# Where the weight sums of a later expert pair stand among the evictions of a batch's first second-layer product

## Chip, cores and metric

The kernel runs on one core of a Trainium2 chip. The metric is the device time of one execution in microseconds, given as the median of several runs. Five engines work on their own instruction queues and meet at semaphores: TensorE (PE, matmuls, and PEld, its weight loads), VectorE (DVE), ScalarE (ACT), GpSimd (POOL) and SyncE (SP, which issues the transfers here).

## What is computed

Three stages follow one another: clustered attention, a gated layer, and a mixture of four experts. The change lies in the last one, so only that is shown:

```python
def _moe2_ref(x, domain_probs, w1, w2):          # x: 1536 x 512, w1: 4 x 512 x 1024, w2: 4 x 1024 x 512
    p = domain_probs / (domain_probs.sum(-1, keepdims=True) + 1e-09)
    out = np.zeros((N, D), dtype=np.float32)
    for e in range(E):
        h = np.maximum(x @ w1[e], 0.0)
        out += p[:, e:e + 1] * (h @ w2[e])
    return out
```

## The kernel before

The stage (`moe2`) walks over 32 pairs: 2 batches of 768 tokens, 4 experts, 4 groups of 256 hidden units. A pair has a first layer, `hidden(i)`, and a second layer, `outp(i)`. The order of the instructions on each engine is the order in which the Python code issues them, since the stage stands under a manual schedule.

`hidden(i)` computes 256 hidden units for 768 tokens by a scheme with seven products of blocks instead of eight. Each product is six matmuls (two halves of the depth, and three terms, because every number is split into a high and a low part). The products go into four PSUM banks, `ph0` to `ph3`, one buffer each. The first product (line 886) is copied out by ScalarE as `m1` (line 887); the sums `u2` and `u3` are formed by VectorE (lines 890 and 893). The fifth product issued (line 899) adds into the bank of the first, so it comes behind the copy `m1`; the sixth (line 903) writes the bank that `u2` read. ReLU and the split into high and low parts are ScalarE's and VectorE's (lines 877 and 878).

`outp(i)` multiplies the hidden units with the second layer's weights in six tiles of 128 tokens. A tile is six matmuls of 512 columns (lines 931 to 933) into one of four `po` buffers in PSUM; VectorE evicts it, scaled by the token's share of the expert. The first pair of a batch writes the accumulator (line 936), the others add to it (line 938). So tile 4 needs the buffer of tile 0, and tile 5 that of tile 1.

Two lists of side work are woven in. `conv_in2(i)` prepares the first layer's weights of pair i: an entry with four sums on VectorE into the tile `sf` (line 828), and four entries, each a ScalarE copy that makes the high part (line 835) and a GpSimd subtraction that makes the low part (line 836), of which two read `sf`. `sf` has one buffer, so the sums of one pair come behind the subtractions of the pair before. `conv_out2` does the same for the second layer's weights (lines 614 and 615). `outp` takes one entry of its list behind each eviction (lines 942 and 943), and issues what is left behind its loop (lines 944 and 945).

The loop over i (lines 950 to 965) issues the load of pair i+2, `hidden(i)`, and then `outp(i-1)` with the list of pair i+2. At i = 0 and i = 16 there is no `outp`; the list of pair i+2 is kept as `late`, and goes into `hidden(1)` or `hidden(17)` behind its own work, whose last entries are issued at its end (lines 910 and 911). So in `hidden(1)` pair 2's weights are prepared, and in `outp(0)`, which follows, pair 3's. In the second batch it is `hidden(17)` with pair 18 and `outp(16)` with pair 19.

Of the kernel before, what the change touches and what calls it, by code (L numbers as in the profile page):

```python
# [69 lines left out]
class Net:  # L70
# [781 lines left out]
    def moe2(self):  # L852
        nc = self.nc
        pairs, hs, acc = self.pairs2, {}, {}
        LAST, PER = len(pairs), len(pairs) // B
# [57 lines left out]
        def outp(i, work=()):  # L913
            work = list(work)
            b, e, g = pairs[i]
            first, last = i % PER == 0, i % PER == PER - 1
            if first:
                acc[b] = self.a2p.tile([128, NT, DM], F32, name="acc2", tag="acc2") if b == 0 else \
                    self.accp.tile([128, NT, DM], F32, name="acc3", tag="acc")
            Hh, Hl = hs.pop(i)  # L920
            wo = self.wout2.pop(i)
            for t in range(NT):

                parts = (slice(0, 256), slice(256, 512)) if i == LAST - 1 and t == NT - 1 else (slice(0, 512),)
                c = slice(t * 128, t * 128 + 128)
                pe = self.pn[:, b, t, e:e + 1]
                for dc in parts:
                    ps = self.ps3.tile([128, 512], F32, name="po2", tag="po")[:, 0:dc.stop - dc.start]
                    for f in range(2):
                        wh, wl = wo[f]  # L930
                        nc.tensor.matmul(ps, Hh[:, f, c], wh[:, dc], start=f == 0, stop=False)  # L931
                        nc.tensor.matmul(ps, Hh[:, f, c], wl[:, dc], start=False, stop=False)  # L932
                        nc.tensor.matmul(ps, Hl[:, f, c], wh[:, dc], start=False, stop=f == 1)  # L933
                    a = acc[b][:, t, dc]
                    if first:
                        nc.vector.tensor_scalar(a, ps, pe, None, op0=ALU.mult)  # L936
                    else:
                        nc.vector.scalar_tensor_tensor(a, ps, pe, a, op0=ALU.mult, op1=ALU.add)  # L938
                    if last:
                        o = self.out[b * S:(b + 1) * S].rearrange("(p t) d -> p t d", t=NT)[:, t, dc]  # L940
                        nc.sync.dma_start(out=o, in_=a)
                if work:
                    work.pop(0)()
            for go in work:
                go()


        sums, split = self.operands(1, [self.block(0, k, n) for k in range(2) for n in range(2)])
        late = []
        for i in range(LAST):  # L950
            if i + 2 < LAST:
                self.load_in2(i + 2)
            hidden(i, (self.conv_out2(i + 1) if i + 1 < LAST else []) + late)
            late = []
            cin = self.conv_in2(i + 2) if i + 2 < LAST else []
            if i + 2 < LAST:
                self.load_out2(i + 2)
            if i == PER - 1:

                outp(i - 1, [lambda o=o: split(o, nc.gpsimd if o in (1, 3) else nc.vector) for o in (0, 4, 1, 5)] + cin[:1])  # L960
                outp(i, [lambda: split(3, nc.gpsimd), lambda: split(6), lambda: split(2)] + cin[1:])
            elif i == 0 or i == PER:
                late = cin
            else:
                outp(i - 1, cin + (sums[i - 2:i - 1] if 2 <= i < 6 else []))
        outp(LAST - 1)

    def run(self):
# [85 lines left out]
```

## Time and profile before

| | us |
|---|---|
| median of 3 runs | 1085.11 (1084.38 to 1086.39) |
| the profiled execution | 1084.51 |
| its span on the core | 1082.6 |
| TensorE busy in the span | 1051.1 (97%) |
| VectorE busy in the span | 773.5 (71%) |
| mean granted TensorE clock, as a share of full speed | 0.991 |

The span is what the trace covers; 1.9 us of the execution lie around it. Times in the rows count from the span's start. A timeline row gives start, length, engine, line, operation, what is written from what, how many instructions were merged into the row, and in brackets the idle time before it with what ended it. Matmuls overlap, so a matmul's length is more than the distance to the next start.

### The profile page before, as it was taken

To read this page: it belongs to the slowest core of one execution; us is meant where nothing else is said; L and a number is where in the kernel's file an instruction comes from. 1 tells how busy PE (TensorE), PEld (TensorE's weight loads), DVE (VectorE), ACT (ScalarE), POOL (GpSimd) and SP (SyncE) were. 2 spreads that over 40 slices of the span, in tenths; PEclk is the share of its full clock that TensorE was granted. 3 is DMA by queue.
4 is the path that set the end of the run, shared out by engine and by line. 5 is a ranking of instruction groups with operands and counts; after the bars stand their busy time and mean duration, and the time that the engine had idled before them with its cause. 6 is when DMAs were issued, how large, how long until landed. Compare 5 with 4: busy or idle time off the path is not lost.

```text
span 1082.6 us, 15421 instructions
## 1 busy us (share of the span) xinstructions
PE 1051.1 (97%) x5621; PEld 947.8 (88%) x5621; DVE 773.5 (71%) x1315; ACT 512.0 (47%) x1060; POOL 465.2 (43%) x398
## 2 busy tenths in 40 slices
PE   6999999999999999999999999999999899999998
PEld 5898999998888888888898888998899798899887
DVE  6998989998877526644357777667768767776765
ACT  4888888888665315503224333333343333333320
POOL 7577787763333103100025444444435544444430
PEclk8999999999999999999999999999999899999999
DMA  8678667655433202102012122212213212221201
GB/s 176 136 160 174 143 150 169 149 131 162 147 117 98 78 1 95 61 1 68 11 40 66 52 78 78 67 50 78 79 59 117 76 42 78 78 72 46 78 20 59
DMA packets 92619, 95.80 MB, mean 88 GB/s; under 512 B 42720, under 2 KB 71744, under 8 KB 92544
## 3 DMA queue, kind: packets, MB, share of 16 engines
q1 hardware_dynamic: 92112, 94.77, 32.2%
q8 instruction: 44, 0.72, 0.3%
q14 instruction: 31, 0.25, 0.1%
q10 hardware_dynamic: 432, 0.06, 0.0%
HBM read 65.07 MB, written 3.19 MB: 63 GB/s over the span
## 4 chain that ended last, share of the span: by engine, by line
PE 83%; DVE 7%; DMA 4%; ACT 3%; POOL 2%; issue 1%; SPq 1%; ACTq 0%; POOLq 0%
PE ph L869 20%; PE po L931 8%; PE po L932 8%; PE po L933 8%; PE S L421 4%; PE T L441 4%; PE pg L621 3%; PE pg L623 3%; PE pv L623 3%; PE pv L621 3%; PE pv L622 3%; PE pg L622 3%; PE po L621 3%; PE po L623 3%; PE po L622 3%; DMA R<-hik 2%
## 5 line engine op out<-in xcount | busy, mean ns | idle before, releaser
L869 PE MATMUL ph<-X,w1h 128*128 128x384 f32 x896 | 229.2, 337 | 0.1
L869 PEld LDWEIGHTS ph<-X,w1h 128*128 128x128 f32 x896 | 163.5, 189 | 3.3 <-DVE h2l L878 0.8
L931 PE MATMUL po<-woh,h2h 128*128 128x512 f32 (+1 forms) x386 | 151.2, 392 | 7.3 <-DVE acc L936 7.3
L938 DVE SCALAR_TENSOR_TENSOR acc<-po,pn,acc 128x512 f32<-128x512 f32 (+1 forms) x181 | 129.8, 742 | 36.3 <-PE po L933 36.3
L615 POOL TENSOR_TENSOR wol<-r,woh 128x512 fp32r<-128x512 f32 x64 | 83.3, 1303 | 168.5 <-ACT woh L614 168.5
L933 PE MATMUL po<-woh,h2l 128*128 128x512 f32 (+1 forms) x386 | 151.5, 392 | 0.0
L932 PE MATMUL po<-wol,h2h 128*128 128x512 f32 (+1 forms) x386 | 151.4, 392 | 0.0
L869 PE MATMUL ph<-X,w1l 128*128 128x384 f32 x448 | 150.6, 336 | 0.0
L596 POOL TENSOR_TENSOR cvc<-cvc,cvs 128x512 int32<-128x512 int32 x36 | 49.5, 1380 | 197.2 <-DVE cvc L593 192.5
L877 ACT ACTIVATE h2h<-ph 128x384 fp32r<-128x384 f32 x128 | 62.6, 490 | 117.5 <-PE ph L869 91.7
L445 DVE TENSOR_TENSOR pl<-T,ph 128x384 fp32r<-128x384 f32 x192 | 97.0, 547 | 13.8 <-ACT ph L444 12.0
L836 POOL TENSOR_TENSOR w1l<-sf,w1h 128x512 fp32r<-128x512 f32 x64 | 81.5, 1296 | 48.1 <-ACT w1h L835 48.1
L836 POOL TENSOR_TENSOR w1l<-r,w1h 128x512 fp32r<-128x512 f32 x64 | 66.9, 1047 | 80.3 <-ACT w1h L835 80.3
L878 DVE SCALAR_TENSOR_TENSOR h2l<-ph,h2h 128x384 fp32r<-128x384 f32 x128 | 71.0, 554 | 34.5 <-ACT h2h L877 31.4
L931 PEld LDWEIGHTS po<-woh,h2h 128*128 128x128 f32 x386 | 73.1, 189 | 22.5 <-DVE acc L936 8.2
L424 DVE TENSOR_REDUCE nm<-S 128x1 f32<-128x768 f32 x96 | 91.1, 949 | 2.0 <-PE S L421 1.1
L421 PE MATMUL S<-R,L 80*128 80x384 f32 (+1 forms) x384 | 92.0, 362 | 0.0
L444 ACT ACTIVATE ph<-T 128x384 fp32r<-128x384 f32 x192 | 84.2, 493 | 16.1 <-PE T L441 15.4
L432 ACT ACTIVATE P<-S,nm 128x768 f32<-128x768 f32 x96 | 87.5, 911 | 3.8 <-DVE nm L424 3.8
L933 PEld LDWEIGHTS po<-woh,h2l 128*128 128x128 f32 x386 | 73.1, 189 | 15.2
L932 PEld LDWEIGHTS po<-wol,h2h 128*128 128x128 f32 x386 | 73.1, 189 | 14.3
L441 PE MATMUL T<-ident,P 128*128 128x128 f32 x576 | 82.4, 277 | 2.8 <-DVE pl L445 2.5
(183 smaller groups left out, 2281.1 us busy)
## 6 DMA issues: line engine op xcount, KB each, us to landing
r<-in_moe_w_dram SPq DMA_DIRECT2D x64, 512.0 KB, 3.8
L<-hiq SPq DMA_DIRECT2D x32, 192.0 KB, 4.7
R<-hik SPq DMA_DIRECT2D x32, 192.0 KB, 4.7
wo<-in_moe_w_out_dram SPq DMA_DIRECT2D x12, 512.0 KB, 3.4
wv<-in_moe_w_val_dram SPq DMA_DIRECT2D x12, 512.0 KB, 4.0
wg<-in_moe_w_gate_dram SPq DMA_DIRECT2D x12, 512.0 KB, 4.6
nq<-in_q_dram SPq DMA_DIRECT2D x16, 192.0 KB, 4.0
nk<-in_k_dram SPq DMA_DIRECT2D x16, 192.0 KB, 4.1
```

The lines of the kernel that those rows point to most:

```text
L421: nc.tensor.matmul(ps[:, a, 0:384], l[0:k, c], r[0:k, a * 384:a * 384 + 384], start=l is L1, stop=l is L2)
L441: nc.tensor.transpose(ps[:, j, :], pt[:, c:c + 128], self.ident)
L445: nc.vector.tensor_tensor(lo, ps, hi.bitcast(F32), op=ALU.subtract)
L621: nc.tensor.matmul(ps, wh, xh, start=first, stop=False)
L622: nc.tensor.matmul(ps, wh, xl, start=False, stop=False)
L623: nc.tensor.matmul(ps, wl, xh, start=False, stop=last)
L836: nc.gpsimd.tensor_tensor(lo[:, sl], x, hi[:, sl].bitcast(F32), op=ALU.subtract)
L869: nc.tensor.matmul(ps, w[:, a, j], y[:, o, j], start=first and j == 0 and k == 0, stop=j == 1 and k == 2, skip_group_check=not first)
L931: nc.tensor.matmul(ps, Hh[:, f, c], wh[:, dc], start=f == 0, stop=False)
L932: nc.tensor.matmul(ps, Hh[:, f, c], wl[:, dc], start=False, stop=False)
L933: nc.tensor.matmul(ps, Hl[:, f, c], wh[:, dc], start=False, stop=f == 1)
L938: nc.vector.scalar_tensor_tensor(a, ps, pe, a, op0=ALU.mult, op1=ALU.add)
```

## The change

In the two calls `outp(0)` (i = 1) and `outp(16)` (i = 17) three empty entries are put ahead of the list. `outp` takes one entry behind each eviction, so the four sums are issued behind the fourth eviction instead of the first, the first weight split behind the fifth and the second behind the sixth, and the last two splits behind the loop. All other calls of `outp` keep their lists.

```diff
@@ -962,7 +962,9 @@
             elif i == 0 or i == PER:
                 late = cin
             else:
-                outp(i - 1, cin + (sums[i - 2:i - 1] if 2 <= i < 6 else []))
+
+                gap = [lambda: None] * (3 if i in (1, PER + 1) else 0)
+                outp(i - 1, gap + cin + (sums[i - 2:i - 1] if 2 <= i < 6 else []))
         outp(LAST - 1)
```

## Rows read from the trace of the kernel before

**Rows 1.** The page's first part: busy us, share of the span, instructions of each engine.

```profile
PE 1051.1 (97%) x5621; PEld 947.8 (88%) x5621; DVE 773.5 (71%) x1315; ACT 512.0 (47%) x1060; POOL 465.2 (43%) x398
```

**Rows 2.** TensorE's waits, whole run: line, releaser, us in total, times, longest.

```profile
PE po L931 <- DVE acc L936: 7.3, 2, 3.7
...
```

**Rows 3.** Busy time and granted clock (PEclk) from one `outp` start to the next.

```profile
core 0: us, PE busy (x) PEld busy (x) DVE busy (x) ACT busy (x) POOL busy (x), PEclk, DMA share, GB/s
585.83:606.60 20.77, 17.09 (x80) 14.97 (x80) 14.20 (x24) 7.57 (x16) 12.17 (x11) 0.92 0.16 51
606.60:622.11 15.51, 15.51 (x80) 14.07 (x80) 11.82 (x21) 5.49 (x12) 7.13 (x7) 1.00 0.23 69
839.53:861.36 21.83, 18.16 (x79) 16.03 (x79) 14.20 (x24) 7.56 (x16) 11.87 (x11) 0.84 0.14 49
861.36:876.87 15.51, 15.51 (x80) 14.07 (x79) 10.95 (x20) 5.49 (x12) 7.13 (x7) 1.00 0.22 68
...
```

**Rows 4.** TensorE's timeline at `outp(0)`: end of tile 4, tile 5, `hidden(2)`.

```profile
592.44 0.39 PE L933 MATMUL po<-woh,h2l 128*128 128x512 f32 x1
596.51 0.79 PE L931 MATMUL po<-woh,h2h 128*128 128x512 f32 x1 [3.67 <-DVE acc L936]
...
599.23 0.59 PE L869 MATMUL ph<-X,w1h 128*128 128x384 f32 x2
...
```

**Rows 5.** TensorE's timeline, an undisturbed pair: first matmuls of `hidden(3)` and of `outp(2)`.

```profile
614.80 0.51 PE L869 MATMUL ph<-X,w1h 128*128 128x384 f32 x2
...
622.10 0.39 PE L931 MATMUL po<-woh,h2h 128*128 128x512 f32 x1
...
```

**Rows 6.** TensorE's timeline at `outp(16)`: end of tile 4, tile 5, `hidden(18)`.

```profile
846.14 0.39 PE L933 MATMUL po<-woh,h2l 128*128 128x512 f32 x1
850.21 0.79 PE L931 MATMUL po<-woh,h2h 128*128 128x512 f32 x1 [3.67 <-DVE acc L936]
...
852.93 0.84 PE L869 MATMUL ph<-X,w1h 128*128 128x384 f32 x2
...
```

**Rows 7.** VectorE's timeline from the end of `hidden(1)` to the sums of pair 4.

```profile
588.07 1.39 DVE L828 TENSOR_TENSOR sf<-sf,r 128x256 f32<-128x256 f32 x1
...
590.05 0.74 DVE L936 TENSOR_SCALAR acc<-po,pn 128x512 f32<-128x512 f32 x1
592.79 0.93 DVE L828 TENSOR_TENSOR sf<-r 128x256 f32<-128x256 f32 x1 [2.00 <-POOL w1l L836]
593.75 1.37 DVE L828 TENSOR_TENSOR sf<-sf,r 128x256 f32<-128x256 f32 x1
...
595.72 2.71 DVE L936 TENSOR_SCALAR acc<-po,pn 128x512 f32<-128x512 f32 x4
...
609.05 1.01 DVE L828 TENSOR_TENSOR sf<-r 128x256 f32<-128x256 f32 x1
...
```

**Rows 8.** GpSimd's timeline at `outp(0)`.

```profile
590.20 2.56 POOL L836 TENSOR_TENSOR w1l<-sf,w1h 128x512 fp32r<-128x512 f32 x2 [1.03 <-ACT w1h L835]
...
595.86 2.51 POOL L836 TENSOR_TENSOR w1l<-sf,w1h 128x512 fp32r<-128x512 f32 x2 [1.02 <-ACT w1h L835]
598.33 0.72 POOL L836 TENSOR_TENSOR w1l<-r,w1h 128x256 fp32r<-128x256 f32 x1
...
```

**Rows 9.** The sums' line 828, whole run: ns min/median/max, and VectorE's idle before it.

```profile
L828 DVE TENSOR_TENSOR sf<-sf,r x32: 424/426/1391, 541.0 to 1035.4; 128x256 f32<-128x256 f32 x32
...
  POOL w1l L836: 4.0, 2
...
```

**Rows 10.** ScalarE's timeline at `outp(0)` and the start of `hidden(2)`.

```profile
595.15 1.30 ACT L835 ACTIVATE w1h<-sf 128x512 fp32r<-128x512 f32 x2 [3.53 <-DVE sf L828]
596.36 0.40 ACT L835 ACTIVATE w1h<-r 128x256 fp32r<-128x256 f32 x1
600.55 0.49 ACT L887 ACTIVATE m<-ph 128x384 f32<-128x384 f32 x1 [3.79 <-PE ph L869]
...
```

**Rows 11.** SyncE's queue: the load of pair 4's first-layer weights.

```profile
593.47 0.37 SPq L808 DMA_DIRECT2D r<-in_moe_w_dram  x1
...
```

**Rows 12.** The page's transfers, whole run: count, KB each, median us to landing.

```profile
r<-in_moe_w_dram SPq DMA_DIRECT2D x64, 512.0 KB, 3.8
...
```

## What the change should do to the time

> **What bounds the kernel now.** I read the page's table of busy shares first [rows 1]: TensorE is busy in 97% of the span and no other engine above 71%, so time can come back only where TensorE stands still or runs at its lower clock. Next the list of waits of TensorE, longest first [rows 2]: its head is a matmul of the second layer that waits for an eviction of line 936, 7.3 us in 2 times. Line 936 evicts only the first pair of a batch, so the two times should be the first second-layer product of each batch, `outp(0)` and `outp(16)`. To size the whole loss I then cut the span from the start of one `outp` to the start of the next [rows 3]. An undisturbed cut is 15.51 us, in both batches, at a granted clock of 1.00; the two cuts that begin at `outp(0)` and `outp(16)` are 20.77 and 21.83 us at 0.92 and 0.84. The excess is 5.26 and 6.32 us, 11.58 us in all. That is more than the wait, so I split it by the timelines of TensorE.
>
> First place [rows 4]: the last matmul of tile 4 starts at 592.44. An undisturbed tile of `outp` takes (614.80 - 606.60)/6 = 1.367 us [rows 3, 5], a matmul of it 0.228, so tile 5 was due at 592.67; it starts at 596.51, 3.84 late. Tile 5 itself takes 596.51 to 599.23 = 2.72 us, twice 1.367: the lower of the clock's two levels, 1.2 instead of 2.4 GHz, right behind an idle of 3.67 us. The following `hidden(2)` lasts to 606.60, 7.37 against 622.10 - 614.80 = 7.30 [rows 3 to 5]. Sum 3.84 + 1.35 + 0.07 = 5.26. Second place [rows 6]: tile 5 was due at 846.37, starts at 850.21 (3.84), takes 2.72 (1.35 too much), and `hidden(18)` 852.93 to 861.36 = 8.43 (1.13 too much): 6.32. Of the 11.58 us, 7.68 are idle and 3.90 the clock behind it.
>
> Why tile 5 waits: `po` has four buffers, so tile 5 needs the eviction of tile 1. VectorE's timeline [rows 7] shows eviction 0 at 590.05, then nothing until 592.79, then the four weight sums of pair 3, and only at 595.72 the evictions 1 to 4. The sums waited for GpSimd, whose two splits of pair 2 that read the one `sf` buffer run 590.20 to 592.76 [rows 8]; over the run this wait counts 4.0 us in 2 times [rows 9]. Eviction 1 ends at about 595.72 + 0.74 = 596.46, and TensorE goes on at 596.51.
>
> **The change, part by part.** Nothing is added: the three empty entries issue no instruction. In `outp(0)` and `outp(16)` the sums go behind eviction 3, the first split behind eviction 4, the second behind eviction 5, the last two behind the loop. The splits are ScalarE copies and GpSimd subtractions; neither engine has anything else in `outp`, so the order inside both queues is what it was. SyncE's queue is untouched too. What changes is VectorE's order alone: four sums trade places with evictions 1 to 3.
>
> Evictions 1 to 3 no longer stand behind the sums. The block of four takes 2.71 us [rows 7]; as one of them is 0.74 long, each starts (2.71 - 0.74)/3 = 0.66 behind the other. So 590.05, 590.71, 591.37, 592.03, and the last ends at 592.77. Their tiles are there: tile 3 begins 3 x 1.367 behind the cut at 585.83 [rows 3], and its last matmul ends near 591.5. Tile 5 is due at 592.67 and needs eviction 1, done at 591.45: 1.2 us of slack. The wait goes in full. With the idle gone the clock has no reason to fall: from `outp(1)` on, without an idle, it is 1.00 [rows 3]. Gain 5.26 and 6.32 us. As the second place has 1.06 us of clock cost more at the same idle, another execution may have it the other way: 2 x 5.26 = 10.5 to 2 x 6.32 = 12.6 are the ends for this term; I take the measured sum, 11.58.
>
> What the sums pay: nothing. They could not start before GpSimd's end at 592.76, whoever stands ahead of them, and eviction 3 ends at 592.77. So they run 592.79 to 595.72 as before, cover and price unchanged, and eviction 4 begins at 595.72, eviction 5 at 596.38 (end 597.12).
>
> What is late next is `hidden(2)`, which TensorE now starts at 592.67 + 1.37 = 594.04 instead of 599.23, while ScalarE and VectorE are still at the sums' consequences. Each product of six matmuls takes 7.30/7 = 1.043 us. On ScalarE, pair 3's splits keep their times, 595.15 to 596.76 [rows 10]; the copy `m` of the first product stands behind them in the queue and runs 596.77 to 597.26 (0.49 [rows 10]). TensorE needs it for the fifth product, which adds into the same bank, at 594.04 + 4 x 1.043 = 598.21: 0.95 us of slack. VectorE does `u2` behind both `m` and eviction 5, 597.3 to 597.9; the sixth product, into the bank `u2` reads, is due at 599.25: 1.4 us of slack. So the covers hold, but the smallest is under 1 us. If evictions and splits slow each other, it is this slack that is eaten first.
>
> That can be bounded by rows. A VectorE sum with two inputs in SBUF does collide with GpSimd: 1.39 us at 588.07 where others take 0.42 [rows 7, 9]. Evictions read PSUM, and do not: the block of four runs at 595.72 to 598.43 beside two GpSimd splits that take 2.51 us, where two splits with only one eviction beside them took 2.56 [rows 7, 8]. I take zero, the row of exactly this pair of operations. The upper end is that GpSimd is locked out for three evictions, 3 x 0.66 = 2.0 us: the sums begin 2.0 later, `m` too, and TensorE loses 2.0 - 0.95 = 1.05 us per place. The lower end (a gain) is excluded, since GpSimd's times set the sums either way.
>
> The Trainium skill, page "SBUF — State Buffer" (section on the two separate sides), says that VectorE and GpSimd share a port pair as an exclusive lock, held by whichever begins first, for two-input SBUF operations and the two-port modes. Read for the sums it agrees with the 1.39 us row; read for every VectorE operation it would be the upper end above, but the same page exempts an operation with at most one SBUF input outside those modes, and the 2.51 us row agrees with the exemption. By the lock the sum would be 9.5 us of gain, by the exemption 11.6.
>
> Transfers: pair 4's weights are issued at 593.47, when GpSimd has freed the buffer, and land in about 3.8 us [rows 11, 12], near 597.3; their sums move from 609.05 [rows 7] to 603.8. Hidden by 6 us. GpSimd, which ends pair 3's splits at 599.05 as before [rows 8], falls behind `hidden(2)` by at most 2 to 3 us; in an undisturbed cut it is busy 7.13 of 15.51 us [rows 3], so it catches up in the same pair.
>
> Sum: 1084.51 (the profiled execution, span 1082.6 and 1.9 around it) - 11.58 = 1072.93. The median of the three runs is 1085.11, 0.60 above this execution: 1073.5 from there. I say 1073.2.
>
> **The rivals.** (a) GpSimd is held up by the evictions and `hidden` gives 1.05 us back at each place: 11.58 - 2.1 = 9.5, time 1075.0 to 1075.6. For it: the two do collide in sums. Against: the 2.51 us row. (b) Only the idle goes and the clock falls anyway, since something else lowers it: gain 7.7, time 1076.8 to 1077.4. Against: 1.00 in the undisturbed cuts. (c) No change: tile 5 does not wait for eviction 1 but for something that also waits for GpSimd; then the idle stays and the time is 1085. Against: 596.46 and 596.51 agree within 0.05 us, and the sums had ended 0.7 us before. (d) Slower: the wait moves from tile 5 into `hidden`. `m` stands behind the splits that stand behind the sums; if the sums end late, TensorE idles at the fifth product, and the clock falls in front of 18 matmuls of `hidden` and 36 of `outp`. At an idle of 5 us and 1.35 to 2.48 us for the clock as now, each place would cost 6.4 to 7.5 where it costs 5.26 and 6.32 today: 1 to 3.4 us slower in all, 1086 to 1088.5. It decides from the point where `m` ends 0.95 + 5 = 6 us later than 597.26. For it: `hidden` now overlaps the sums, which it did not before. Against: nothing in GpSimd's or ScalarE's queue moves.
>
> **How the numbers follow.** Forecast (whole gain) 0.84, (a) 0.08, (b) 0.04, (c) 0.02, (d) 0.02. A measurement of this kernel tells about 0.2%, 2.2 us, from no change; forecast, (a) and (b) are all faster than that: 0.96; (c) within 0.2% with the mild part of (d): 0.03; slower 0.01. Low end: the lowest run, 1084.38, less 12.6 = 1071.8. High end: the highest run, 1086.39, less 9.4 = 1077.0, which takes in (a) and most of (b).
>
> **What would show it.** Right: no wait of TensorE for line 936; four evictions in a row ahead of the sums, the sums still at GpSimd's end; both cuts near 15.5 us at a clock of 1.00. Wrong in (a): splits longer than 1.3 us each beside evictions and an idle ahead of the fifth product of `hidden(2)`. Wrong in (b): matmuls of 0.63 us in `outp(0)` without an idle ahead. Wrong in (d): a wait of TensorE for ScalarE's `m` or VectorE's `u`, with half-clock matmuls behind it.

## The result, and the profile after

| | before | after |
|---|---|---|
| median, us | 1085.75 (1084.38 to 1087.13, 4 runs) | 1073.18 (1071.80 to 1075.07, 4 runs) |
| ratio | | 0.9887, 95% interval 0.9859 to 0.9915 |
| the profiled execution and its span, us | 1084.51, 1082.6 | 1073.04, 1071.1 |
| mean granted TensorE clock | 0.991 | 0.996 |

The change takes 1.1% off. By the medians that is 12.57 us, by the two profiled executions 11.47; the runs of either kernel spread over some 3 us. TensorE's waits over the whole run (line, releaser, us in total, times, longest) now begin with entries of the attention stage; the wait for line 936 that headed [rows 2] is in the list no more:

```profile
PE oT L364 <- DVE oh L358: 5.0, 1, 5.0
PE PV L454 <- ACT U L461: 5.0, 7, 1.2
...
```

The same cuts as in [rows 3], from one `outp` start to the next, of the changed kernel (length, busy time and count of PE, PEld, DVE, ACT, POOL, then the clock):

```profile
585.85:601.35 15.50, 15.50 (x79) 14.05 (x79) 14.14 (x24) 7.45 (x16) 12.29 (x11) 1.00 0.20 69
601.35:616.86 15.51, 15.51 (x79) 14.06 (x79) 11.81 (x21) 5.48 (x12) 7.12 (x7) 1.00 0.23 69
834.31:849.82 15.51, 15.51 (x79) 14.06 (x79) 14.15 (x24) 7.46 (x16) 11.93 (x11) 1.00 0.21 69
849.82:865.33 15.51, 15.51 (x80) 14.07 (x80) 10.94 (x20) 5.48 (x12) 7.11 (x7) 1.00 0.22 68
...
```

The cuts of `outp(0)` and `outp(16)` are as long as the undisturbed ones, with TensorE busy all through and the clock at 1.00. They lost 20.77 - 15.50 = 5.27 and 21.83 - 15.51 = 6.32 us, together 11.59, where the span lost 11.5. Nothing of it came back later: VectorE is busy 14.14 us of the first cut, as much as before, but no longer in TensorE's way.

TensorE's timeline at `outp(0)` (answers to [rows 4]): end of tile 4, tile 5, first and fifth product of `hidden(2)`, and the start of `outp(1)`:

```profile
592.46 0.39 PE L933 MATMUL po<-woh,h2l 128*128 128x512 f32 x1
592.69 0.39 PE L931 MATMUL po<-woh,h2h 128*128 128x512 f32 x1
...
594.05 0.51 PE L869 MATMUL ph<-X,w1h 128*128 128x384 f32 x2
...
598.23 0.51 PE L869 MATMUL ph<-X,w1h 128*128 128x384 f32 x2
...
601.35 0.39 PE L931 MATMUL po<-woh,h2h 128*128 128x512 f32 x1
...
```

No row carries an idle time in brackets. VectorE's (answers to [rows 7]):

```profile
590.07 2.71 DVE L936 TENSOR_SCALAR acc<-po,pn 128x512 f32<-128x512 f32 x4
592.81 0.94 DVE L828 TENSOR_TENSOR sf<-r 128x256 f32<-128x256 f32 x1
593.78 1.40 DVE L828 TENSOR_TENSOR sf<-sf,r 128x256 f32<-128x256 f32 x1
...
595.77 1.40 DVE L936 TENSOR_SCALAR acc<-po,pn 128x512 f32<-128x512 f32 x2
597.24 0.56 DVE L890 TENSOR_TENSOR u<-m,ph 128x384 f32<-128x384 f32 x1
...
603.80 1.00 DVE L828 TENSOR_TENSOR sf<-r 128x256 f32<-128x256 f32 x1
...
```

Four evictions fill the 2.7 us in which VectorE did one eviction and then stood for 2.00 us before, and the sums begin at 592.81 where they began at 592.79. GpSimd's and ScalarE's (answers to [rows 8, 10]):

```profile
590.22 2.55 POOL L836 TENSOR_TENSOR w1l<-sf,w1h 128x512 fp32r<-128x512 f32 x2 [1.03 <-ACT w1h L835]
...
595.92 2.56 POOL L836 TENSOR_TENSOR w1l<-sf,w1h 128x512 fp32r<-128x512 f32 x2 [1.03 <-ACT w1h L835]
598.42 0.75 POOL L836 TENSOR_TENSOR w1l<-r,w1h 128x256 fp32r<-128x256 f32 x1
599.12 2.73 POOL L615 TENSOR_TENSOR wol<-r,woh 128x512 fp32r<-128x512 f32 x2
...
```

```profile
595.21 1.30 ACT L835 ACTIVATE w1h<-sf 128x512 fp32r<-128x512 f32 x2 [3.57 <-DVE sf L828]
...
596.73 0.48 ACT L887 ACTIVATE m<-ph 128x384 f32<-128x384 f32 x1
...
```

The two `sf` splits take 2.55 us beside four evictions, as they took 2.56 beside one. GpSimd reaches the splits of the second layer's weights (line 615) only at 599.12, straight behind its own work, and ends them by 601.85; its next row, at 603.24, waits for ScalarE again, so it has caught up.

### The profile page after: what moved, and what is told of

Same layout as the page of the kernel before. It is cut to its first block, busy times and chain, and to the rows that moved or that the text cites. A ratio compares the mean times of both kernels' runs of the same rounds, so it can differ in the third digit from the quotient of the medians.

```text
span 1071.1 us, 15421 instructions
## 1 busy us (share of the span) xinstructions
PE 1046.2 (98%) x5621; PEld 943.0 (88%) x5621; DVE 778.4 (73%) x1315; ACT 511.8 (48%) x1060; POOL 464.4 (43%) x398
## 4 chain that ended last, share of the span: by engine, by line
PE 88%; DVE 5%; DMA 3%; ACT 2%; SPq 1%; issue 1%; POOL 0%; ACTq 0%; DVEq 0%; POOLq 0%
PE ph L869 21%; PE po L932 8%; PE po L933 8%; PE po L931 8%; PE T L441 4%; PE S L421 4%; PE pg L621 3%; PE po L621 3%; PE po L622 3%; PE po L623 3%; PE pg L622 3%; PE pv L622 3%; PE pv L621 3%; PE pg L623 3%; PE pv L623 3%; PE PV L454 2%
```

## The experiments

In all of them, two cuts are the measure: the one that begins at `outp(0)` and the one that begins at `outp(16)`, 15.50 us undisturbed. The total time alone is a coarser one, because the stages ahead of the mixture do not always take as long (last section).

**Behind the second eviction.** One empty entry instead of three, so only eviction 1 stands ahead of the sums:

```diff
-                gap = [lambda: None] * (3 if i in (1, PER + 1) else 0)
+                gap = [lambda: None] * (1 if i in (1, PER + 1) else 0)
```

> One empty entry instead of three: in outp(0) and outp(16) the four sums stand behind the second eviction, so only eviction 1 is moved ahead of them. My theory (tile 5 waits for eviction 1 alone): the whole gain, 1073 us, and no idle of TensorE at line 931; evictions 2 to 5 then run behind the sums and end near 598.4 on the trace's time, u2 by 599.0, just ahead of the sixth product of hidden(2) due at 599.25, so at most 0.3 us is lost per place. Rival (each eviction moved ahead of the sums brings its share): about a third of 12 us, 1081 us.

Measured: 1075.17 us, ratio to before 0.9914 (0.9882 to 0.9946). Both places' cuts, then VectorE at the first place, where `outp(0)` began at 587.37:

```profile
587.37:603.00 15.63, 15.63 (x80) 14.03 (x79) 13.93 (x24) 7.56 (x16) 12.56 (x11) 1.00 0.24 68
...
835.90:851.54 15.64, 15.64 (x80) 14.03 (x80) 13.92 (x24) 7.46 (x16) 12.04 (x11) 1.00 0.25 68
...
```

```profile
591.60 1.40 DVE L936 TENSOR_SCALAR acc<-po,pn 128x512 f32<-128x512 f32 x2
594.33 0.94 DVE L828 TENSOR_TENSOR sf<-r 128x256 f32<-128x256 f32 x1 [1.33 <-POOL w1l L836]
...
597.29 2.72 DVE L936 TENSOR_SCALAR acc<-po,pn 128x512 f32<-128x512 f32 x4
599.92 0.54 DVE L890 TENSOR_TENSOR u<-m,ph 128x384 f32<-128x384 f32 x1
...
601.23 0.56 DVE L898 TENSOR_TENSOR ph<-u,ph 128x384 f32<-128x384 f32 x1
...
```

TensorE's weight loads (PEld) at the seventh product of `hidden(2)`:

```profile
601.49 0.19 PEld L869 LDWEIGHTS ph<-X,w1l 128*128 128x128 f32 x1
601.84 0.30 PEld L869 LDWEIGHTS ph<-X,w1h 128*128 128x128 f32 x2 [0.16 <-DVE ph L898]
...
```

One eviction moved brings nearly all: the cuts are 0.13 us longer than behind the fourth. The wait of VectorE for GpSimd is there again (1.33 us), and costs nothing. The 0.13 us stand at the seventh product of `hidden(2)`, which adds into the bank that VectorE's last row reads, and not at the sixth, which was expected to be the tightest. Its weights could load at 601.49 + 0.19 = 601.68, but the load waits for that row, which ends at 601.79, and begins at 601.84, 0.16 us late. So the evictions do not bring equal shares, as the rival had it: moving eviction 1 alone takes TensorE's wait away. Of the 1.65 us by which the profiled execution (1074.69) is above the changed kernel's (1073.04), 1.5 lie ahead of `outp(0)` (587.37 against 585.85).

**Behind the sixth eviction.** The other way: six empty entries, so the sums follow all evictions.

```diff
-                gap = [lambda: None] * (3 if i in (1, PER + 1) else 0)
+                gap = [lambda: None] * (6 if i in (1, PER + 1) else 0)
```

> Six empty entries: the four sums stand behind all six evictions, and all weight splits behind the loop. My theory: evictions 4 and 5 wait for their tiles and end near 595.0; GpSimd has by then ended pair 2's splits, so the sums no longer collide and take 4 x 0.34 us, to about 596.4; m ends near 597.8 where the fifth product of hidden(2) needs it at 598.2. So no idle, the whole gain, 1073 us, and 0.5 us less slack than behind the fourth. Rival (the sums need their place behind the fourth eviction, since every later place holds up hidden): an idle of TensorE at the fifth product of hidden(2) of 1 us or more per place, 1075 to 1080 us.

Measured: 1075.76 us, ratio 0.9907 (0.9875 to 0.9938). Both cuts, then VectorE and GpSimd in the first:

```profile
588.73:604.23 15.50, 15.50 (x79) 14.06 (x79) 12.86 (x24) 7.67 (x16) 11.91 (x11) 1.00 0.20 69
...
837.11:852.62 15.51, 15.51 (x80) 14.07 (x79) 12.76 (x24) 7.46 (x16) 11.28 (x11) 1.00 0.19 69
...
```

```profile
593.06 3.46 DVE L936 TENSOR_SCALAR acc<-po,pn 128x512 f32<-128x512 f32 x5
597.13 0.75 DVE L936 TENSOR_SCALAR acc<-po,pn 128x512 f32<-128x512 f32 x1 [0.61 <-PE po L933]
597.79 0.41 DVE L828 TENSOR_TENSOR sf<-r 128x256 f32<-128x256 f32 x1
...
598.92 0.42 DVE L828 TENSOR_TENSOR sf<-r,sf 128x256 f32<-128x256 f32 x1
...
```

```profile
593.22 2.56 POOL L836 TENSOR_TENSOR w1l<-sf,w1h 128x512 fp32r<-128x512 f32 x2 [1.03 <-ACT w1h L835]
595.73 1.99 POOL L836 TENSOR_TENSOR w1l<-r,w1h 128x256 fp32r<-128x256 f32 x2
...
```

Both cuts are 15.50 to 15.51 us: the whole gain. GpSimd has ended (595.73 + 1.99 = 597.72) when the sums begin, and they take 597.79 to 599.34 = 1.55 us, half of the 3.0 that they take behind the fourth. The place behind the fourth is not special: behind the sixth the gain is the same, and behind the second 0.13 us less at each place.

**One batch at a time.** The three entries in `outp(0)` alone, then in `outp(16)` alone:

```diff
-                gap = [lambda: None] * (3 if i in (1, PER + 1) else 0)
+                gap = [lambda: None] * (3 if i == 1 else 0)
```

> The three empty entries in outp(0) only; outp(16) as in the kernel before. My theory (the places are independent and each pays its idle of 3.84 us and the clock behind it): 5.3 us of gain, about 1080.4 us; the cut that begins at outp(0) is 15.5 us at a granted clock of 1.00, that of outp(16) between 20.8 and 21.9 us. Rival (what is won in the first batch is waited for later): less than 3 us of gain.

```diff
-                gap = [lambda: None] * (3 if i in (1, PER + 1) else 0)
+                gap = [lambda: None] * (3 if i == PER + 1 else 0)
```

> The three empty entries in outp(16) only; outp(0) as in the kernel before. My theory: 5.3 to 6.3 us of gain, 1079 to 1080.5 us; together with the kernel that changes only outp(0) the gains add up to that of the change, 12 us. The cut of outp(0) stays between 20.8 and 21.9 us: should it show the larger clock cost this time, the 1.06 us between the two places belongs to the execution and not to the place. Rival: the gains do not add up, the sum of both is under 9 us.

Measured: 1079.63 us, 0.9947 (0.9930 to 0.9965), and 1080.74 us, 0.9956 (0.9936 to 0.9977), against 1085.3 of the kernel before beside them: 5.7 and 4.6 us, 10.2 together. The 4.6 us of the second batch lie under the 5.3 to 6.3 that were expected; its interval is 2.5 to 6.9 us, so the totals alone would not decide. The cuts do: those of the changed places are 15.50 and 15.51 us. Of the place left as it was, one row from each kernel, `outp(16)` of the first and `outp(0)` of the second:

```profile
834.70:855.73 21.03, 17.35 (x79) 15.22 (x79) 14.19 (x24) 7.56 (x16) 11.88 (x11) 0.92 0.16 51
...
```

```profile
586.38:607.25 20.87, 17.19 (x79) 15.06 (x79) 14.20 (x24) 7.56 (x16) 12.22 (x11) 0.92 0.18 51
...
```

The places are independent, and their gains add up. `outp(16)`, which lost 6.32 us in the kernel before, lost 21.03 - 15.51 = 5.52 here, at the same wait of 3.7 us. So the second place does not always cost the 1.06 us more. But here the first place no longer idles, and the kernel of the next experiment, where both do, again shows the second place higher (cuts of 20.57 and 21.72 us). Whether the difference belongs to the execution or to a second idle behind a first one stays open.

**A second buffer instead of another order.** The kernel before, with the sums behind the first eviction, but pairs 3 and 19 write an `sf` of their own:

```diff
-            sf = t["sf"] = self.sfp.tile([128, 4, 2, 128], F32, name="sf", tag="sf")
+            sf = t["sf"] = (self.sf2 if i in (3, 19) else self.sfp).tile([128, 4, 2, 128], F32, name="sf", tag="sf")
...
         self.a2p = self.pool(es, "a2p")
+        self.sf2 = self.pool(es, "sf2")
```

> The kernel before, with the sums behind the first eviction, but pairs 3 and 19 get an sf buffer of their own, so that their sums need not wait for GpSimd's splits of the pair before. Theory 1 (the wait for sf is the whole cause): the sums run from 590.7 in 1.4 us, eviction 1 ends near 592.9, tile 5 starts 0.3 us late and the whole gain is there, about 1074 us. Theory 2 (mine; without the wait the sums run beside GpSimd's splits, which from 590.2 to 594.8 stand back to back, and a sum with two inputs in SBUF is held up by each of them, as 1.39 for 0.42 us in the trace of before): the sums take 3 to 4.5 us, eviction 1 ends between 594.4 and 596, TensorE still idles 1.7 to 3.3 us at each place, and the cut is 17.2 to 20.8 us; 1076 to 1083 us.

Measured: 1087.01 us against 1087.13, ratio 0.9992 (0.9971 to 1.0013). The first cut, TensorE's wait, VectorE and GpSimd:

```profile
585.67:606.24 20.57, 17.19 (x79) 15.06 (x79) 15.89 (x24) 7.56 (x16) 12.71 (x11) 0.92 0.19 52
...
```

```profile
596.05 0.80 PE L931 MATMUL po<-woh,h2h 128*128 128x512 f32 x1 [3.38 <-DVE acc L936]
...
```

```profile
590.57 1.07 DVE L828 TENSOR_TENSOR sf<-r 128x256 f32<-128x256 f32 x1
591.67 1.39 DVE L828 TENSOR_TENSOR sf<-sf,r 128x256 f32<-128x256 f32 x1
592.99 0.94 DVE L828 TENSOR_TENSOR sf<-r 128x256 f32<-128x256 f32 x1
593.85 1.48 DVE L828 TENSOR_TENSOR sf<-r,sf 128x256 f32<-128x256 f32 x1
595.25 2.71 DVE L936 TENSOR_SCALAR acc<-po,pn 128x512 f32<-128x512 f32 x4
...
```

```profile
590.05 2.73 POOL L836 TENSOR_TENSOR w1l<-sf,w1h 128x512 fp32r<-128x512 f32 x2 [1.03 <-ACT w1h L835]
592.74 2.31 POOL L836 TENSOR_TENSOR w1l<-r,w1h 128x256 fp32r<-128x256 f32 x2
...
```

The wait for `sf` is gone: the first sum starts at 590.57, right behind eviction 0. But the four sums now take 590.57 to 595.33 = 4.76 us where they take 1.55 with GpSimd idle, and the evictions start at 595.25 instead of 595.72. TensorE's idle fell from 3.67 to 3.38 us. All four of VectorE's sums are long while GpSimd's four operations stand back to back. The two take turns: taken one by one, GpSimd's four end at 591.35, 592.79, 593.65 and 595.05, and each sum ends 0.27 to 0.29 us behind one of them. GpSimd's rows last 2.73 + 2.31 us where they last 2.56 + 1.99 without a sum beside them (the kernel with the sums behind the sixth eviction): 0.5 us more, against 3.2 for VectorE. So behind the wait for the buffer stood a second barrier, nearly as high. That was theory 2, which put it too low: it expected sums of 3 to 4.5 us, an idle of 1.7 to 3.3 us and a total of 1076 to 1083 us. The Trainium skill, page "SBUF — State Buffer" (section on the two separate sides), says that a VectorE operation with two SBUF inputs and a GpSimd operation that reads SBUF exclude each other for a whole instruction; the four rows agree, and the evictions, which read PSUM, show no such thing (four still take 2.71 us beside GpSimd).

**The slack in `hidden`.** The changed kernel, with n further ScalarE copies behind the last weight split of `outp(0)` and `outp(16)`, ahead of `m`; n is 1, 4 and 9:

```diff
                 outp(i - 1, gap + cin + (sums[i - 2:i - 1] if 2 <= i < 6 else []))
+                if i in (1, PER + 1):
+                    junk = self.tmp.tile([128, 512], F32, name="junk", tag="junk", bufs=1)
+                    for _ in range(4):
+                        nc.scalar.activation(junk, acc[i // PER][:, 0], AF.Copy)
```

> The changed kernel, with one further ScalarE copy of 128x512 at the end of outp(0) and of outp(16), behind the last weight split and ahead of m; its result is used by nobody. It measures the slack of m. m ends 0.6 us later, near 597.8 where the fifth product of hidden(2) needs it at 598.2: no idle, both cuts 15.5 us. Rival (m has no slack, the copy counts in full): cuts of 16.1 us.

> The changed kernel with four such copies at each place: 2.2 to 2.5 us. Of these 1.0 us is slack, so TensorE idles 1.2 to 1.5 us ahead of the fifth product of hidden(2) and hidden(18), and the cuts are 16.7 to 17.0 us if an idle of that length leaves the clock at 1.00; if the clock falls as it does behind 3.67 us, 18 us and more.

> The changed kernel with nine such copies at each place: 5.0 to 5.6 us, of which 1.0 is slack. By the slower rival's mechanism TensorE idles 4.0 to 4.6 us ahead of the fifth product, the clock falls to the lower level behind it, and the cuts are 21 to 22.5 us: what the change gained is given back, about 1084 to 1087 us. If the clock does not fall behind an idle inside hidden: cuts of 19.5 to 20.1 us, about 1082 us.

Measured, with one copy: 1074.44 us in a single run, both cuts 15.51 us; the copy is hidden. With four, 1075.01 us in a single run; the cuts, and ScalarE and TensorE at the first place:

```profile
584.50:601.79 17.29, 15.79 (x80) 14.03 (x79) 14.29 (x24) 10.11 (x20) 12.59 (x11) 1.00 0.19 62
...
834.69:851.87 17.18, 15.80 (x80) 14.03 (x79) 14.16 (x24) 9.88 (x20) 11.97 (x11) 1.00 0.19 62
...
```

```profile
595.51 2.60 ACT L971 ACTIVATE junk<-acc 128x512 f32<-128x512 f32 x4
598.02 0.47 ACT L887 ACTIVATE m<-ph 128x384 f32<-128x384 f32 x1
...
```

```profile
598.55 0.62 PE L869 MATMUL ph<-X,w1h 128*128 128x384 f32 x2 [1.50 <-ACT m L887]
...
```

`m` starts 598.02 - 584.50 = 13.52 us behind the start of `outp(0)`; without copies it is 596.73 - 585.85 = 10.88. So it is 2.64 late, of which 1.79 appear in the cut: the slack is 0.85 us. At the second place `m` starts 13.41 us behind `outp(16)`, 2.53 late, of which 1.67 appear: 0.86. An idle of 1.50 us leaves the clock at 1.00. The cuts are 0.2 to 0.3 us above what was expected, since the copies made `m` up to 2.64 us late, and not 2.2 to 2.5, and the slack is 0.85 us, and not 1.0.

With nine copies: 1088.11 us, ratio 1.0026 (1.0005 to 1.0047), 0.3% slower than the kernel before. Both cuts, then ScalarE and TensorE's wait at the first place:

```profile
584.93:607.47 22.54, 17.86 (x80) 16.10 (x79) 14.38 (x24) 13.24 (x25) 12.63 (x11) 0.85 0.14 48
...
840.37:863.17 22.80, 18.10 (x79) 16.34 (x79) 14.38 (x24) 13.26 (x25) 12.44 (x11) 0.85 0.15 47
...
```

```profile
601.64 0.47 ACT L887 ACTIVATE m<-ph 128x384 f32<-128x384 f32 x1
...
```

```profile
602.16 1.01 PE L869 MATMUL ph<-X,w1h 128*128 128x384 f32 x2 [4.68 <-ACT m L887]
...
```

`m` is 16.71 - 10.88 = 5.83 us late, 5.0 past the slack, and the cuts are 7.0 and 7.3 us too long: some 2.0 to 2.3 us are the clock's, at 0.85 of full speed over the cut. That is a little more than expected (cuts of 21 to 22.5 us, 1084 to 1087 us), as nine copies made `m` 5.8 us late and not 5.0 to 5.6. The slower rival's mechanism exists and has the price that was put on it, 6.4 to 7.5 us a place. The changed kernel stays 0.85 us clear of the point where TensorE begins to wait, and further from the one where the clock falls: it did not behind 1.50 us of idle, and did behind 3.38.

## Why the prediction was right

The time was forecast as 1073.2 us; it is 1073.18. That close a hit is partly luck: the runs spread over 3 us, and the medians differ by 12.57 us where 11.58 were forecast. But the steps hold one by one:

- **The loss.** 5.26 and 6.32 us were read off the cuts; 5.27 and 6.32 came back. Taking the cut rather than the 7.3 us of the list of waits was what mattered: a third of the loss was the lower clock behind the idle, and has no entry among the waits.
- **Where tile 5 waits.** For eviction 1, said the prediction. The kernel with the sums behind the second eviction shows it: one eviction moved ahead, and the idle is gone.
- **The sums pay nothing.** Worked out as 592.79 to 595.72; they run 592.81 to about 595.8. Four evictions and GpSimd's two splits end within 0.01 us of each other (592.78 and 592.77), and the row of the sums shows no wait for either. Evictions and splits do not slow each other, as the 2.51 us row had said; rival (a) falls with 2.55.
- **What is late next.** `m` was put at 596.77 to 597.26 and needed at 598.21; it runs 596.73 to 597.21 and is needed at 598.23. The slack of 0.95 us was then measured as 0.85. `u2` at 597.3 is 597.24; pair 4's sums at 603.8 are at 603.80.
- **The clock.** Rival (b), in which it falls anyway, is refuted: 1.00 in both cuts without an idle ahead.
- **The end 10.5 to 12.6 us** of the gain came from taking the 1.06 us between the two places as something that may differ from execution to execution. That was not shown. The second place did lose only 5.52 us once, but in a kernel whose first place no longer idled; in both profiled executions in which both places idle, it is the second that costs more. The sum of 11.58 held without it.

One step told less than the whole cause. The prediction named the wait for GpSimd's splits at the one `sf` buffer, and the collision of the sums with GpSimd as a thing that only bounds a cost. The kernel with the second buffer shows that the collision by itself would have held the evictions until 595.25. Had the change been the second buffer, the list of waits (4.0 us in 2 times, [rows 9]) would have promised a gain that does not come. Not tried: a second buffer together with the new order, which by these rows should bring nothing more.

## What to carry to other kernels

Work that can wait should not stand in an engine's queue between results that free a buffer for the bottleneck engine: find which eviction the waiting tile needs, and put the other work behind that one, wherever it itself was waiting anyway. Read the loss from the length of a repeating cut against an undisturbed one, which has the clock in it, and before the order is changed work out which result is needed next and by how much it is early, here 0.85 us. When a wait is taken away by a buffer instead, look at what the two engines do to each other once they overlap.

## What the runs showed of the hardware that was not expected

- A VectorE sum of two SBUF operands, 0.41 us alone, took 0.94 to 1.48 us in each of four turns beside a busy GpSimd, whose four operations took 2.73 + 2.31 instead of 2.56 + 1.99 us: the two took turns, and VectorE paid 3.2 us of it and GpSimd 0.5.
- The clock's cost behind one and the same idle is not always the same: at 3.67 to 3.68 us of idle the cuts were 5.26, 5.36, 5.52 and 6.32 us too long, the largest at a second place behind an idle first one. Behind 1.50 us of idle the clock stayed at 1.00.
- The stages ahead of the mixture, the same in all kernels here, ended at different times: `outp(0)` began between 584.50 and 588.73 us in the ten profiled executions. That is over a third of the gain, and the reason why two kernels with equal cuts differ by up to 2.7 us in their profiled executions. From 300 to 584 us all ten run alike (TensorE busy 283.93 us, clock 1.00), so the difference arises in the first 300 us; what sets it there stays open.
